# Attention with a routed feed-forward on one core: a value bank for each half of the queries

## The chip, the core and the metric

The kernel runs on one core of a Trainium2 chip. The time is the device time of one execution in microseconds; the figure for a kernel is the median of its runs. TensorE (PE in the profile) does matmuls and transposes, VectorE (DVE) and ScalarE (ACT) work on the results, GpSimd (POOL) does small work and indirect transfers, and SyncE (SP) issues most of the transfers. Matmul results land in PSUM, which is divided into banks of 512 fp32 values per partition.

## What is computed

Attention over 8 batches of 8 heads, 576 rows and 64 columns, in which each row keeps only the scores within `tau` of its maximum; then a mixture of 8 experts, in which every expert takes up to 576 rows by a greedy choice over all gate logits:

```python
def _attn_ref(q, k, v, tau):
    scale = 1.0 / np.sqrt(q.shape[-1])
    scores = scale * np.matmul(q, k.transpose(0, 1, 3, 2))
    thresh = np.max(scores, axis=-1, keepdims=True) - tau
    scores = np.where(scores >= thresh, scores, -1000000000.0)
    scores = scores - np.max(scores, axis=-1, keepdims=True)
    attn = np.exp(scores)
    attn = attn / (np.sum(attn, axis=-1, keepdims=True) + 1e-09)
    return np.matmul(attn, v).astype(np.float32)
...
def _moe_ref(x, w_gate, w1, w2):
...
    for e in range(E):
        mask = assigned == e
        h = np.maximum(x[mask] @ w1[e], 0.0)
        out[mask] = h @ w2[e]
```

## The kernel before, in words

The program has an attention stage, a short passage in which the router's first search runs beside the last gathered rows, and eight rounds of the expert feed-forward. The change lies in the attention stage and in the order of work right behind it.

**Pairs, tiles, slots.** Two heads of a batch make a pair: 32 pairs, four to a batch. A pair has nine tiles: eight of 128 query rows of one head, and a ninth that holds the last 64 rows of both heads. The 288 tiles go through a pipeline written out by hand in the loop over slots (lines 287 to 315); a slot starts two tiles, so nine slots handle two pairs and 18 slots a batch. In one slot the following are issued, each for the two tiles that have come that far:

- TensorE: scores (`score`, line 69) into a tile `sc` of two banks, one per tile; there are two such tiles, so the scores of a slot need the readers of the slot before to be done. At the slot's end the transposes of the weighted rows (`tr` and `turn`, line 98) into `tb`, of which there is one.
- VectorE: `mx` (line 74) reads the scores, writes `z` and the row's extreme; then `stt` (line 90) masks and sums the rows of the two tiles from a slot earlier.
- ScalarE: `trev` (lines 113 and 115) copies the transposed rows of the slot before to `pt`, then `ex` (line 86) takes the exponentials of this slot's `z`.

**Value units.** The output of a pair is formed in two halves of the query columns, 256 and 320 wide (`FQ`). A half takes four value units (`pv_unit`, line 144, two matmuls each) that accumulate into a bank `xo`, and the leftover matmuls (`pl_unit`, line 152) that finish both halves; ScalarE copies both banks to `xt` (line 153) in the next slot. The leftover matmuls need the leftover keys in `pl`: ten small transposes per pair (`left`, line 117, by `turn`) into unused columns of the score tiles, and four copies by ScalarE (`leftev`, lines 123 to 127).

**Whole units.** When the four pairs of a batch are done, `finish` puts four gate units (`lg_unit` twice, lines 171 and 173; `lgt_unit`, 183; `lgm_unit`, 193) into the list `aux`, and for the first two batches five row units as well (`xt_unit`, line 205: four transposes of `xt`, a copy and a store). The rows of the other batches wait until after the stage, in `late`. Each takes a bank `xo`, and its results are read by ScalarE or VectorE in the next slot.

**What sets the order.** Both kinds share a pool of two banks (`ps_v`, line 32). `columns` (line 257) takes value units from the queue, evenly over the slots that are left to a pair (`last_slot`); it doesn't open a pair's first half while whole units are waiting and no half is open, with exceptions. `whole` (line 271) issues up to two whole units in a slot, but only while no half is open:

```python
    def free_v(): return len(banks)<2 or banks[-2][0]
...
                if first and (not free_v() or (not all and not XO and len(aux)>(3 if p%2 else 0) and st["held"]!=p)): return
...
        while n<2 and aux and not XO and free_v() and st["slot"]>=st["last"]+aux[0][0]:
```

In the slot after a pair's ninth tile was transposed, all ten leftover transposes are issued: six behind the first tile's scores, four behind the second's, and ScalarE's four copies of them stand ahead of both exponentials.

Of the kernel before, what the change touches and what calls it, by code (L numbers as in the profile page):

```python
# [22 lines left out]
def attention(ctx, tc, qk, vl, tau, wgd, xrows, xts, Lg, nb_batches, ident, swap, R, after_first):  # L23
# [8 lines left out]
    ps_v=ctx.enter_context(tc.tile_pool(name="ps_v",bufs=2,space=PSUM))  # L32
# [89 lines left out]
    def leftev(p,n):  # L122
        if n==0: a=LB.pop((p,0)); A.activation(PL[p][:,0:384].rearrange("p (g r q) -> p r g q",g=3,r=2),a[:,:,HS:HS+192].rearrange("p r (g q) -> p r g q",g=3),AF.Copy)  # L123
        if n==0: return
        b=LB.pop((p,1))
        A.activation(PL[p][:,384:512].rearrange("p (r q) -> p r q",r=2),b[:,:,HS:HS+64],AF.Copy)
        for r in range(2): A.activation(PL[p][64-64*r:128-64*r,512:576],b[64-64*r:128-64*r,r,HS+64:HS+128],AF.Copy)  # L127
# [5 lines left out]
    banks=[]; VB={}  # L133
    def bank_v(sh):
        t=ps_v.tile(sh,F32,name="xo"); banks.append([False]); VB[id(t)]=banks[-1]
        return t
    def free_v(): return len(banks)<2 or banks[-2][0]
    def pv_unit(p,f,u):
        b,j=divmod(p,4)
        if b not in XT: XT[b]=wk.tile([128,4,S],F32,name="xt",bufs=XTB)  # L140
        if u==0: XO[p,f]=bank_v([128,512])
# [3 lines left out]
    def pl_unit(p,fs=(0,1)):  # L145

        b,j=divmod(p,4); r=[]
        for f in fs:
            xo=XO.pop((p,f)); q=FQ[f]; n=q.stop-q.start
            for a in range(2):  # L150
                g=slice(64*a,64*a+64); h=a^f
                T.matmul(xo[64*h:64*h+64,:n],LD[p]["v"][g,f,512:576],PL[p][g,q],start=False,stop=True,skip_group_check=True)  # L152
            r.append((VB[id(xo)],lambda xo=xo,q=q,n=n: A.activation(XT[b][:,j,q],xo[:,:n],AF.Copy)))
        have[p,"pv"]=1
        return r
    def bank_g(b,sh):
        if b<nb_batches-1: return bank_v(sh)
# [43 lines left out]
    def xt_unit(b,c):  # L201
        ps=bank_v([128,4,128])
# [20 lines left out]
    queue=[]; aux=[]; later=[]; late=[]; late2=[]; st={"last":-9,"slot":0,"held":-1}  # L223
    def push_pair(p):
        b,j=divmod(p,4)
        def when(n): return lambda: have.get((p,n),1<<30)+HOLD<=st["slot"]
        if p==NP-1:
# [4 lines left out]
            for f in range(2):  # L232
                for u in range(4): queue.append(("c",when("t3" if f==0 else "t8"),u==0,lambda f=f,u=u: pv_unit(p,f,u),p))
# [3 lines left out]
            queue.append(("n",lambda: not later,False,lambda: late.extend([lambda c=c: xt_unit(b,c) for c in range(5)]),p))  # L237
            return
        for f in range(2):
            for u in range(4): queue.append(("c",when("t3" if f==0 else "t8"),u==0,lambda f=f,u=u: pv_unit(p,f,u),p))  # L240
# [5 lines left out]
    def finish(b):  # L246
        aux.extend([(0,lambda: lg_unit(b,0)),(0,lambda: lg_unit(b,1)),(1,lambda: lgt_unit(b)),(0,lambda: lgm_unit(b))])
        rows=[lambda c=c: xt_unit(b,c) for c in range(5)]
# [7 lines left out]
    def last_slot(p): return 9*(p//2)+(12 if p%2 else 8)  # L256
# [700 lines left out]
```

## Time and profile before

| | us |
|---|---|
| median of three runs (1012.51 to 1014.81) | 1012.78 |
| the profiled execution | 1014.5 |
| its span, from the first to the last instruction | 1012.7 |
| busy in the span: PE, DVE, ACT, POOL | 960.3, 784.7, 639.1, 258.7 |
| first and last row-maximum instruction of attention start | 5.4, 468.9 |

The page gives busy times of each engine; groups of instructions by source line with their count, busy time, mean length and the idle time of their engine just before them; and who waited for whom. In the timeline the first column is the start and the second the length, both in us from the span's start, then the engine, the line, the operation, what is written and read, and how many were merged. A bracket gives the idle time before and what ended it. PEld is TensorE's weight load, which runs beside its matmuls.

### The profile page before, as it was taken

What the parts mean: (1) busy time and instruction counts of PE and PEld (TensorE: products, weight loads), DVE (VectorE), ACT (ScalarE), POOL (GpSimd) and SP (SyncE); (2) the same over time, 40 slices, a digit from 0 to 9 for tenths busy, and PEclk for the clock granted to TensorE, in tenths of its full rate; (3) what the DMA queues carried; (4) which work ended last, traced back from release to release, by engine and by line L of the source; (5) the groups of instructions that cost most, each with busy time, mean ns of one, the idle gap of its engine ahead of it and who ended that gap; (6) DMA issues with size and microseconds to landing.
All of it is one profiled execution on the core that took longest, in us unless ns stands there. A gap on an engine that the chain in (4) does not pass through costs nothing.

```text
span 1012.7 us, 24106 instructions
## 1 busy us (share of the span) xinstructions
PE 960.3 (95%) x9141; PEld 704.5 (70%) x9141; DVE 784.7 (77%) x2158; ACT 639.1 (63%) x1257; POOL 258.7 (26%) x411
## 2 busy tenths in 40 slices
PE   7999999999999999999879999999999899999996
PEld 4555555555555555555669789797887879899895
DVE  7999999999999899997578788788687687525220
ACT  6898889788988889897745344254352444535340
POOL 2333433333333333232020222221221203220202
PEclk9999999999999999999979999999999999999999
DMA  6332424233432323202770523434343415351101
GB/s 247 98 116 83 140 81 157 99 135 124 169 115 95 102 101 118 95 26 88 245 250 13 170 97 121 136 114 128 124 138 115 143 50 177 93 174 53 42 11 41
DMA packets 35859, 116.99 MB, mean 116 GB/s; under 512 B 4384, under 2 KB 5024, under 8 KB 35232
## 3 DMA queue, kind: packets, MB, share of 16 engines
q1 hardware_dynamic: 28352, 92.85, 26.8%
q0 software_dynamic: 5888, 19.03, 6.0%
q10 hardware_dynamic: 1504, 3.59, 1.2%
q8 instruction: 72, 1.18, 0.5%
q14 instruction: 43, 0.35, 0.1%
HBM read 93.01 MB, written 21.38 MB: 113 GB/s over the span
## 4 chain that ended last, share of the span: by engine, by line
PE 69%; DVE 12%; ACT 10%; issue 6%; DMA 2%; another core or an unknown queue 0%; DVEq 0%; POOLq 0%; SPq 0%; ACTq 0%
PE pf L787 21%; PE pf L819 19%; PE xo L144 8%; PE sc L69 8%; PE tb L98 6%; DVE z L74 4%; ACT pp L86 4%; DVE pp L90 3%; ACT pt L113 3%; PE xo L152 2%; PE pt L732 2%; ACT pl L127 1%; PE rps L440 1%; PE xo L205 1%; DMA out_dram<-y,idx 1%
## 5 line engine op out<-in xcount | busy, mean ns | idle before, releaser
L75 POOL TENSOR_SCALAR nb<-nb,taub 128x1 f32<-128x1 f32 x288 | 149.4, 519 | 308.3 <-DVE z L74 257.6
L74 DVE TENSOR_SCALAR_CACHE_REDUCE z<-sc 128x576 f32<-128x576 f32 x288 | 205.9, 752 | 26.8 <-PE sc L69 14.1
L86 ACT ACTIVATE pp<-z,nb 128x576 f32<-128x576 f32 x256 | 186.4, 771 | 23.6 <-DVE z L74 23.6
L90 DVE SCALAR_TENSOR_TENSOR pp<-z,nb,pp 128x576 f32<-128x576 f32 x256 | 199.9, 813 | 0.3
L819 PE MATMUL pf<-w2h,H 128*128 128x512 f32 x576 | 195.3, 402 | 0.7 <-DVE H L372 0.7
L69 PE MATMUL sc<-qk 64*128 64x288 f32 (+1 forms) x1280 | 186.4, 427 | 7.2 <-ACT pl L123 2.7
L144 PE MATMUL xo<-pt,vt 128*64 128x320 f32 (+1 forms) x1024 | 151.1, 418 | 3.4 <-PE sc L69 1.2
L113 ACT ACTIVATE pt<-tb 128x512 f32<-128x512 f32 x256 | 139.0, 588 | 5.2 <-PE tb L98 2.2
L819 PE MATMUL pf<-w2l,H 128*128 128x512 f32 x320 | 128.3, 401 | 0.0
L826 POOL DMA_INDIRECT out_dram<-y,idx x40 | 44.6, 1115 | 314.6 <-ACT y L822 238.6
L98 PEld LDWEIGHTS tb<-ident,pp 64*128 64x128 f32 x2048 | 75.0, 139 | 69.6 <-ACT pt L113 28.0
L819 PEld LDWEIGHTS pf<-w2h,H 128*128 128x128 f32 x576 | 106.5, 189 | 20.2 <-DVE H L372 1.6
L69 PEld LDWEIGHTS sc<-qk 64*128 64x128 f32 (+1 forms) x1280 | 91.1, 178 | 34.3 <-ACT pl L127 9.0
L787 PE MATMUL pf<-xh,w1h 128*128 128x288 f32 (+2 forms) x512 | 110.7, 303 | 0.7 <-ACT xh L733 0.7
L144 PEld LDWEIGHTS xo<-pt,vt 128*64 128x64 f32 x1024 | 63.4, 136 | 68.4 <-issue 34.7
L787 PE MATMUL pf<-xh,w1l 128*128 128x288 f32 (+2 forms) x512 | 110.7, 302 | 0.0
L787 PE MATMUL pf<-xl,w1h 128*128 128x288 f32 (+2 forms) x512 | 110.6, 302 | 0.0
L98 PE MATMUL tb<-ident,pp 64*128 64x64 f32 x2048 | 93.9, 229 | 12.3 <-ACT pt L113 12.0
L822 ACT ACTIVATE y<-pf 128x512 f32<-128x512 f32 x40 | 23.9, 598 | 129.3 <-PE pf L819 121.1
L799 ACT ACTIVATE hf<-pf 128x576 f32<-128x576 f32 x56 | 36.5, 652 | 93.2 <-PE pf L787 80.3
L787 PEld LDWEIGHTS pf<-xh,w1h 128*128 128x128 f32 x512 | 82.6, 191 | 1.5 <-ACT xh L733 1.1
L787 PEld LDWEIGHTS pf<-xh,w1l 128*128 128x128 f32 x512 | 82.6, 191 | 0.2
(199 smaller groups left out, 1311.4 us busy)
## 6 DMA issues: line engine op xcount, KB each, us to landing
qk<-qk_dram SPq DMA_DIRECT2D x31, 864.0 KB, 4.9
vt<-vl_dram SPq DMA_DIRECT2D x32, 576.0 KB, 3.8
w2s<-w_dram SPq DMA_DIRECT2D x32, 512.0 KB, 5.3
w1s<-w_dram SPq DMA_DIRECT2D x28, 512.0 KB, 4.3
xrows<-pp SPq DMA_DIRECT2D x24, 260.0 KB, 2.3
xts<-xt SPq DMA_DIRECT2D x2, 1152.0 KB
pt<-xts SPq DMA_DIRECT2D x2, 1152.0 KB, 7.9
xrows<-xr SPq DMA_DIRECT2D x8, 260.0 KB, 2.4
```

What stands on the lines that cost most here:

```text
L69: T.matmul(sc[o,f,:HS], kd["q",h][r,c], kd["k",h][r,:],start=True,stop=True)
L74: V.tensor_scalar(z,SC.pop(t)[:,:,:HS],-0.125,None,op0=ALU.mult,op1=ALU.min,accum_out=nb[:,0:1])
L75: G.tensor_scalar(nb[:,1:2],nb[:,0:1],taub[:,0:1],None,op0=ALU.add)
L86: A.activation(pview(t),ZB[t].rearrange("p a b -> p (a b)"),AF.Exp,bias=NBI[t][:,0:1],scale=-1.0)
L90: V.scalar_tensor_tensor(pv,ZB.pop(t).rearrange("p a b -> p (a b)"),NBI[t][:,1:2],pv,op0=ALU.is_le,op1=ALU.mult,accum_out=den_of(p)[:,p%4, ...
L98: g=slice(64*r,64*r+64); T.transpose(o[:,r],x[r%len(x)][g],ident[g,g])
L113: A.activation(PT[p][:,i%2,:,(i//2)*128:(i//2+1)*128].rearrange("p k (r q) -> p r k q",r=2),tb,AF.Copy)
L144: T.matmul(xo[64*h:64*h+64,:q.stop-q.start],v[:,f,128*u+64*h:128*u+64*h+64],PT[p][:,h,u,q],start=(u==0),stop=False,skip_group_check=True)
L787: T.matmul(ps[:,h,:n],s[w][:,k,f*128:(f+1)*128],s[x][:,k,cols[h]],start=(i==0),stop=(i==11))
L799: A.activation(hf,ps[:,:,:HS],AF.Relu)
L819: T.matmul(ps[:,0,:],H[:,f,c:c+128],s[w][:,f],start=(f==0 and j==0),stop=e)
L826: G.indirect_dma_start(out=out,out_offset=IOA(ap=s["idx"][:n,t:t+1],axis=0),in_=y[:n],in_offset=None)
```

## The change

- Each half has its own bank: `xo0` for the first, `xo1` for the second, one buffer each, with a list of flags for each. A first unit waits only for its own bank to be copied out; the hold-back for waiting whole units is gone.
- Whole units take the second half's bank, at most one in a slot, whenever it is free: beside value units of the first half.
- The leftover transposes go in two parts: six in the slot in which the ninth tile is transposed, four a slot later, both behind the scores of both tiles, in the second score tile. ScalarE's copies stand between the two exponentials.
- At the end, the last two pairs are spread over one slot less; in the slots without scores, the transposes go ahead of the value units. The late rows take the two banks in turn.

The names a to i stand for the nine slots of two pairs, counted from the slot in which the leftover keys of the first pair's ninth tile are at the stage of transposition: a and b hold the first pair's leftover transposes after the change (b all ten before), e and f the second pair's (f all ten before), and e and i the leftover matmuls.

```diff
-    ps_v=ctx.enter_context(tc.tile_pool(name="ps_v",bufs=2,space=PSUM))
+    ps_v=ctx.enter_context(tc.tile_pool(name="ps_v",bufs=1,space=PSUM))
...
     def leftev(p,n):
-        if n==0: a=LB.pop((p,0)); A.activation(PL[p][:,0:384]...
-        if n==0: return
-        b=LB.pop((p,1))
+        sc=LB.pop((p,n))
+        if n==0:
+            A.activation(PL[p][:,0:384]...
+            return
...
-    def free_v(): return len(banks)<2 or banks[-2][0]
+    banks=([[True]],[[True]])
+    def bank_v(sh,n):
+        banks[n].append([False])
+        return ps_v.tile(sh,F32,name="xo%d"%n)
+    def free_v(n): return banks[n][-1][0]
...
-        if u==0: XO[p,f]=bank_v([128,512])
+        if u==0: XO[p,f]=bank_v([128,512],f)
...
-        if b<nb_batches-1: return bank_v(sh)
+        if b<nb_batches-1: return bank_v(sh,1)
...
-    def xt_unit(b,c):
-        ps=bank_v([128,4,128])
+    def xt_unit(b,c,k=1):
+        ps=bank_v([128,4,128],k)
...
-    def last_slot(p): return 9*(p//2)+(12 if p%2 else 8)
+    def last_slot(p): return 9*(p//2)+(12 if p%2 else 8 if p<NP-2 else 7)
...
-                if first and (not free_v() or (not all and not XO and len(aux)>(3 if p%2 else 0) and st["held"]!=p)): return
+                if first and not free_v(first-1): return
...
     def whole():
-        n=0
-        while n<2 and aux and not XO and free_v() and st["slot"]>=st["last"]+aux[0][0]:
-            r=aux.pop(0)[1](); n+=1; st["last"]=st["slot"]
-            if queue: st["held"]=queue[0][4]
-            later.append((banks[-1],r))
+        if aux and free_v(1) and st["slot"]>=st["last"]+aux[0][0]:
+            r=aux.pop(0)[1](); st["last"]=st["slot"]
+            later.append((banks[1][-1],r))
...
-        p8=[t//9 for t in ev_ if t%9==8]
-        for n in range(2):
-            if n<len(sc_): score(sc_[n])
-            for p in p8: left(p,n,sc_[n] if n<len(sc_) else None)
+        p8=[(t//9,n) for n,x in enumerate((tr_,ev_)) for t in x if t%9==8]
+        for t in sc_: score(t)
+        for p,n in p8: left(p,n,sc_[-1] if sc_ else None)
...
-        for n in range(2):
-            for p in p8: leftev(p,n)
-        for t in sc_: ex(t)
+        for t in sc_[:1]: ex(t)
+        for p,n in p8: leftev(p,n)
+        for t in sc_[1:]: ex(t)
...
-        columns(); whole()
+        if sc_: columns(); whole()
         for t in tr_: tr(t,t==tr_[0])
+        if not sc_: columns(True); whole()
...
-            now=at; late.pop(0)()(); at=now+XTY
+            now=at; late.pop(0)(len(late)%2)(); at=now+XTY
```

TensorE's instructions in slots a and b of the sixth batch's gate units, before (`sc` scores and, written by `ident`, leftover transposes; `xo` with `wg` and `swap` gate units, with `vt` value units; `tb` transposes of the weighted rows):

```order
L69 MATMUL sc<-qk 128x288 x4
L171 MATMUL xo<-xt,wg 32x256 x4
L173 MATMUL xo<-rd,swap 128x4
L171 MATMUL xo<-xt,wg 32x320 x4
L98 MATMUL tb<-ident,pm_100 128x64 x8
L98 MATMUL tb<-ident,pp 128x64 x8
L69 MATMUL sc<-qk 128x288 x2
L98 MATMUL sc<-ident,pp 128x64 x6
L69 MATMUL sc<-qk 128x288 x2
L98 MATMUL sc<-ident,pp 128x64 x2
L98 MATMUL sc<-ident,pm_100 128x64 x2
L144 MATMUL xo<-pt,vt 64x256 x4
```

The same two slots after the change (lines are shifted by two behind the new code; the numbers tell the two banks' tiles apart):

```order
L69 MATMUL sc<-qk 128x288 x4
L98 MATMUL sc<-ident,pp 128x64 x6
L146 MATMUL xo_5886<-pt,vt 64x256 x2
L173 MATMUL xo_5890<-xt,wg 32x256 x4
L175 MATMUL xo_5890<-rd,swap 128x4
L98 MATMUL tb<-ident,pm_100 128x64 x8
L98 MATMUL tb<-ident,pp 128x64 x8
L69 MATMUL sc<-qk 128x288 x4
L98 MATMUL sc<-ident,pp 128x64 x2
L98 MATMUL sc<-ident,pm_100 128x64 x2
L146 MATMUL xo_5886<-pt,vt 64x256 x4
L173 MATMUL xo_5953<-xt,wg 32x320 x4
```

Slot a now has the first value unit and six leftover transposes, and one gate unit instead of two; slot b has four leftover transposes instead of ten, and the second gate unit.

ScalarE's instructions around the leftover copies of an odd pair (slot f), before (`xt` value copies, `pt` transposed rows, `pl` leftover copies, `pp` exponentials):

```order
L153 ACTIVATE xt<-xo 128x256
L153 ACTIVATE xt<-xo 128x320
L113 ACTIVATE pt<-tb 128x2x4x64
L115 ACTIVATE pt<-tb 128x8x64
L123 ACTIVATE pl<-sc 128x2x3x64
L126 ACTIVATE pl<-sc 128x128
L127 ACTIVATE pl<-sc 64x64 x2
L86 ACTIVATE pp<-z,nb 128x576 x2
```

And after, from the exponentials of slot e to those of slot f:

```order
L86 ACTIVATE pp<-z,nb 128x576
L125 ACTIVATE pl<-sc 128x2x3x64
L86 ACTIVATE pp<-z,nb 128x576
L155 ACTIVATE xt<-xo_831 128x256
L155 ACTIVATE xt<-xo_930 128x320
L113 ACTIVATE pt<-tb 128x2x4x64
L115 ACTIVATE pt<-tb 128x8x64
L86 ACTIVATE pp<-z,nb 128x576
L127 ACTIVATE pl<-sc 128x128
L128 ACTIVATE pl<-sc 64x64 x2
L86 ACTIVATE pp<-z,nb 128x576
```

The large copy moved a slot ahead, and both parts stand behind the first exponential.

TensorE's instructions at the end of the stage, from the last scores on, before:

```order
L69 MATMUL sc<-qk 64x288 x4
L144 MATMUL xo<-pt,vt 64x256 x4
L98 MATMUL tb<-ident,pp 128x64 x16
L144 MATMUL xo<-pt,vt 64x320 x4
L98 MATMUL tb<-ident,pp 128x64 x16
L144 MATMUL xo<-pt,vt 64x320 x4
```

And after:

```order
L69 MATMUL sc<-qk 64x288 x4
L146 MATMUL xo_7349<-pt,vt 64x320 x4
L98 MATMUL tb<-ident,pp 128x64 x32
L146 MATMUL xo_7349<-pt,vt 64x320 x4
```

Four value matmuls of the first half went ahead of the last scores, and two slots' transposes now follow each other.

More of the change, by code (lines that the diff above doesn't have):

```diff
@@ L217, in xt_unit @@
         return ev
-    queue=[]; aux=[]; later=[]; late=[]; late2=[]; st={"last":-9,"slot":0,"held":-1}
+    queue=[]; aux=[]; later=[]; late=[]; late2=[]; st={"last":-9,"slot":0}
     def push_pair(p):
@@ L232, in push_pair @@
             for f in range(2):
-                for u in range(4): queue.append(("c",when("t3" if f==0 else "t8"),u==0,lambda f=f,u=u: pv_unit(p,f,u),p))
+                for u in range(4): queue.append(("c",when("t3" if f==0 else "t8"),0 if u else f+1,lambda f=f,u=u: pv_unit(p,f,u),p))
                 if f==0: queue.append(("n",when("t8"),False,lambda: rd_calc(b),p))
@@ L282, in attention @@
     after_first()
-    ps=ps_v.tile([128,512],F32,name="xo")
+    ps=bank_v([128,512],0); banks[0][-1][0]=True
     def idles(n):
```

18 lines of the change are left out of this document (7 added, 11 removed).

## The prediction

> **What bounds the kernel now.** I read the groups of instructions first, then the waits, then the stretches, then the timeline of the attention stage, where all of the change lies. VectorE's group for the row maxima (`z`, line 74), from the page:
>
> ```profile
> L74 DVE TENSOR_SCALAR_CACHE_REDUCE z<-sc 128x576 f32<-128x576 f32 x288 | 205.9, 752 | 26.8 <-PE sc L69 14.1
> ```
>
> Behind the bar stands 26.8 us of idle time ahead of these 288 instructions. The waits (engine, line, awaited: us in total, times, longest) name its causes and two more that matter below:
>
> ```profile
> DVE z L74 <- PE sc L69: 14.1, 21, 3.4
> DVE z L74 <- PE sc L98: 11.6, 15, 0.8
> ACT pl L123 <- DVE z L74: 24.0, 29, 2.1
> PE tb L98 <- ACT pt L113: 12.7, 32, 1.0
> ```
>
> `z` waits for scores (L69), or for the leftover transposes (L98 into `sc`); TensorE's own transposes wait 32 times, 0.4 us on average, for ScalarE. One stretch of 40 us in the stage (busy us of each engine, granted clock, DMA):
>
> ```profile
> 380.00:420.00 40.00, 37.74 (x449) 21.98 (x449) 37.14 (x104) 35.29 (x66) 11.81 (x24) 1.00 0.32 101
> ```
>
> TensorE 37.74, VectorE 37.14 and ScalarE 35.29 of 40 us, at full clock: three engines nearly full, with two or three microseconds lost in each 40. None is the bound all the time; TensorE and VectorE alternate. The timeline of two slots (start, us, engine) shows how:
>
> ```profile
> 356.12 0.71 PE L98 MATMUL tb<-ident,pp 64*128 64x64 f32 x16
> 356.66 1.19 PE L69 MATMUL sc<-qk 64*128 64x288 f32 x8
> 357.42 0.76 DVE L74 TENSOR_SCALAR_CACHE_REDUCE z<-sc 128x576 f32<-128x576 f32 x1
> 357.78 1.30 PE L144 MATMUL xo<-pt,vt 128*64 128x320 f32 x8
> 359.01 0.77 PE L152 MATMUL xo<-pl,vt 64*64 64x256 f32 x8
> 359.71 0.71 ACT L153 ACTIVATE xt<-xo 128x256 f32<-128x256 f32 x2
> 359.71 0.46 PE L98 MATMUL tb<-ident,pp 64*128 64x64 f32 x8
> 360.26 0.70 PE L69 MATMUL sc<-qk 64*128 64x288 f32 x4
> 360.80 0.34 PE L98 MATMUL sc<-ident,pp 64*128 64x64 f32 x6
> 360.98 0.70 PE L69 MATMUL sc<-qk 64*128 64x288 f32 x4
> 361.18 0.76 DVE L74 TENSOR_SCALAR_CACHE_REDUCE z<-sc 128x576 f32<-128x576 f32 x1 [0.84 <-PE sc L98]
> 361.52 0.22 PE L98 MATMUL sc<-ident,pp 64*128 64x64 f32 x2
> 361.73 1.08 PE L144 MATMUL xo<-pt,vt 128*64 128x256 f32 x8
> 362.04 0.49 ACT L123 ACTIVATE pl<-sc 128x384 f32<-128x384 f32 x1 [0.49 <-DVE z L74]
> 362.75 0.71 PE L98 MATMUL tb<-ident,pp 64*128 64x64 f32 x16
> 363.29 1.19 PE L69 MATMUL sc<-qk 64*128 64x288 f32 x8
> ```
>
> TensorE is packed, so costs are start to start (the trace counts each fp32 matmul that is no transpose twice: x8 is four). Scores of two tiles: 357.78-356.66 = 1.12. Transposes of two tiles: 356.66-356.12 = 0.54 (0.55 below). Four value matmuls of the second half 359.01-357.78 = 1.23, of the first half 362.75-361.73 = 1.02. Leftover value matmuls (L152) 359.71-359.01 = 0.70. Leftover transposes: six 0.18 (360.80 to 360.98), four 0.21 (361.52 to 361.73). `z` starts 357.42-356.66 = 0.76 after the scores when it waits for them. At 361.18 it has waited 0.84 us: the slot before was 3.6 us of TensorE work, and the six transposes ran between its own scores and it. ScalarE's `pl` copy at 362.04 comes before the exponentials, and holds the score tile it reads.
>
> Gate units on TensorE (L171 and L173; then L183 and L193):
>
> ```profile
> 374.20 0.64 PE L171 MATMUL xo<-xt,wg 128*32 128x256 f32 x8
> 374.77 0.39 PE L173 MATMUL xo<-rd,swap 128*128 128x4 f32 x2
> 375.08 0.74 PE L171 MATMUL xo<-xt,wg 128*32 128x320 f32 x8
> 375.76 0.46 PE L98 MATMUL tb<-ident,pm 64*128 64x64 f32 x8
> 344.73 0.66 PE L183 MATMUL xo<-ident,lt 128*128 128x128 f32 x4
> 345.42 0.46 PE L98 MATMUL tb<-ident,pm 64*128 64x64 f32 x8
> ```
>
> The first gate unit costs 0.57+0.31 = 0.88, the second 0.68, the two transposed ones 0.69 (about 0.49 and 0.20). On VectorE:
>
> ```profile
> 366.89 0.17 DVE L164 TENSOR_SCALAR rd<-den 128x36 f32<-128x36 f32 x1
> 367.40 0.70 DVE L74 TENSOR_SCALAR_CACHE_REDUCE z<-sc 128x576 f32<-128x576 f32 x1
> 370.24 0.76 DVE L74 TENSOR_SCALAR_CACHE_REDUCE z<-sc 128x576 f32<-128x576 f32 x1
> 376.68 0.36 DVE L178 COPY rm<-rd 64x4 f32<-64x4 f32 x2
> 377.42 0.76 DVE L74 TENSOR_SCALAR_CACHE_REDUCE z<-sc 128x576 f32<-128x576 f32 x1
> 347.21 0.48 DVE L188 TENSOR_TENSOR lw<-xo,rd 128x128 f32<-128x128 f32 x2
> 348.69 0.74 DVE L74 TENSOR_SCALAR_CACHE_REDUCE z<-sc 128x576 f32<-128x576 f32 x1
> 137.28 1.09 PE L205 MATMUL xo<-ident,xt 128*128 128x128 f32 x8
> 139.75 1.28 DVE L213 COPY xr<-xo 128x512 f32<-128x512 f32 x2
> ```
>
> A slot without extras takes VectorE 370.24-367.40 = 2.84. Each batch adds the reciprocal 0.51 (366.89 to 367.40), the `rm` copies 0.74 (376.68 to 377.42) and the logits 1.48 (347.21 to 348.69): 2.73. A row unit takes TensorE 1.09/2 = 0.55 and VectorE 1.28/2 = 0.64; ten of them run inside the stage. The ends of the stretch that I sum, slots 16 and 142 of the 144:
>
> ```profile
> 50.74 0.75 DVE L74 TENSOR_SCALAR_CACHE_REDUCE z<-sc 128x576 f32<-128x576 f32 x1
> 461.09 0.76 DVE L74 TENSOR_SCALAR_CACHE_REDUCE z<-sc 128x576 f32<-128x576 f32 x1 [0.67 <-PE sc L69]
> ```
>
> 126 slots, seven batches of 18, in 410.35 us, or 58.6 a batch. VectorE's work in it is 126x2.84 + 7x2.73 + 10x0.64 = 383.4 us; the other 27.0 are waits.
>
> **The change part by part.** No matmul, copy or exponential is added or dropped in these slots; what changes is which slot holds them. I name the nine slots of two pairs a to i, as in the section on the change. TensorE's work, with 1.67 for scores and transposes in each:
>
> Before, without gates: a 1.67, b 3.08 (ten leftover transposes, 1.02), c 2.69, d 2.90, e 1.67+1.23+0.70 = 3.60, f 3.08, g 2.69, h 2.90, i 3.60. All gate units lie in a (1.56 or 0.69) or, where the hold-back misses, in f together with those transposes.
>
> After: a 1.67+0.18+0.51 = 2.36, b 1.67+0.21+1.02 = 2.90, c 1.67+0.51+0.62 = 2.80, d 2.90, e 1.67+0.18+0.62+0.70 = 3.17, f 2.90, g 2.69, h 2.90, i 3.60. Gate units go to a (0.88), b (0.68), f (0.49), g (0.20), one in each.
>
> The sums are equal; the spread is not. TensorE can run ahead of VectorE by only 2.84-0.76-0.76 = 1.3 us, since the two score tiles must be read before they are refilled, and lead beyond that is lost. Tally of the lead through a changed batch, starting at none; each slot adds VectorE's time less TensorE's, and what would go under zero is a wait. Gate half: a 2.84-3.24 = -0.40, wait 0.40; b 2.84+0.74-3.58 = 0; c +0.04; d -0.06, wait 0.02; e -0.33, wait 0.33; f 2.84-3.39 = -0.55, wait 0.55; g 2.84+1.0-2.89 = +0.95; h +0.42, to the cap 1.3; i -0.76, to 0.54. Other half: a +0.48, b -0.06, c +0.04, d -0.06, e -0.33, f -0.06, g +0.15+0.51 and h -0.06 leave 1.15, i 0.39. That lead then covers the next batch's a, all but 0.01, so a settled batch waits 0.01+0.02+0.33+0.55 = 0.91 us and takes 18x2.84 + 2.73 + 0.91 = 54.8. TensorE's own sum is 28.5+26.2 = 54.7: it would be dense. The two batches with row units add 5x0.55 to TensorE: 57.4, and VectorE has 57.1; I take 57.6. Seven batches: 5x54.8 + 2x57.6 = 389.2, against 410.35: **21.2 us less**.
>
> The leftover copies. Their transposes now stand behind both score tiles, in the second. So the first `z` of a slot no longer waits for them, and of the two score tiles only the second waits for ScalarE. The second `z` starts at the earliest 0.76+0.76 = 1.52 after the scores began, the six transposes end at 1.12+0.34 = 1.46: no wait. The page of the Trainium skill "PSUM — Partial Sum Buffer", section "PSUM bank collisions raise a hardware error", asks for accesses of two engines to be kept apart by bank, not by address. By it the transposes still share a bank with what `z` reads, and only the 0.06 us above keeps the saving whole; the trace agrees that they are kept apart, with `z` at 361.18 behind transposes that end at 360.80+0.34 = 361.14.
>
> What I keep back. ScalarE is busy 35.29 of 40 us, some 2.5 of a slot of 2.9, and slot f has the two `xt` copies (0.71) and the rest of `pl` on top, so the transposes of slot g may still wait for it as they do now (0.4 us, once a pair). The waits for `pl` ahead of the scores go, so I leave half of that 0.4, 0.2 us, in 16 slots: 3.2 us. From nothing (21.2 stays) to all 12.7 us as now (8.5 stays). **I take 18.0 us.**
>
> Row units. Each leaves with its own VectorE copy in the next slot, 0.64, where two came together; POOL's part and the store go along. On SP's queue the stores now stand between other loads, but those loads are issued a pair or more ahead. Nothing, at most 10x0.64 within what the tally holds.
>
> The end. The value matmuls of one group (1.02) move ahead of the last scores, and one set of transposes ahead of the value matmuls. The row there:
>
> ```profile
> 472.25 0.71 PE L98 MATMUL tb<-ident,pp 64*128 64x64 f32 x16 [0.35 <-ACT pt L113]
> ```
>
> TensorE waits 0.35 for ScalarE even with those matmuls ahead of it, so without them it waits longer: from nothing to 1.02, I take **0.3**. Late rows alternate between two banks as they did, and the router's search behind them is the same chain; it starts earlier by what the stage saves.
>
> The sum: the profiled execution took 1014.5 us (span 1012.7) and stands 1.7 over the median of 1012.78. 1014.5-18.3 = 996.2 for it; **994.5 us** for the median.
>
> **The rivals.** A measurement of this kernel can tell about 0.3% (3 us) from no change.
>
> *ScalarE becomes the bound.* Its 12.7 us of holding TensorE's transposes stay in full, since `pl` copies now sit between two exponentials. For it: 35.29 of 40 busy. Against: the queue gets shorter where it was longest. 21.2-12.7 = 8.5 gained: 1004.3 us.
>
> *Slower: one bank for each half.* Before, groups rotated over two banks; now the next group of a half must wait for its own bank's copy, and all transposes and scores queue behind it on TensorE. A bank's two `xt` copies take 0.71, at most 0.36 on average for one. If all 64 group starts, 28 gate units and 10 row units waited as long as a copy, 102x0.36 = 37 us are lost: 994.5+37 = 1031 us, and it turns the balance at 18.3/102 = 0.2 us each. Against: in the rows above the copies end at 359.71+0.71 = 360.42, and the next group starts at 361.73, 1.3 us later. It decides only if ScalarE falls 1.3 us further behind. The Trainium skill's "Perfetto Trace Analysis", section "Matmuls", says that independent groups should rotate through banks so that the copy-out overlaps the next group: by that rule the change goes the wrong way within a half. The trace bears it out only as far as groups of one half followed each other directly, which they don't.
>
> *Nothing gained.* VectorE is full, and the lead that TensorE gains is spent in slots where VectorE has its extras. Its 27.0 us of waits speak against; for it, the lead is capped at 1.3 us. Within 3 us: 1012 us.
>
> *All of it and more.* No wait for ScalarE is left, and the start and the end give 1 to 3 us besides: 989 us.
>
> **How the numbers follow.** Forecast (990 to 999 us) 0.70; ScalarE as the bound (999 to 1009.7) 0.15; more (under 990) 0.07; nothing 0.04; slower 0.04. Faster: 0.70+0.15+0.07 = 0.92, same 0.04, slower 0.04. The range reaches from 988.5, where nearly all of the fourth case is in, to 1005, just past the ScalarE case.
>
> **What would show it.** Right: the 126 slots take about 392 us; idle time ahead of `z` falls from 26.8 to 10 us or less, with L98 gone from its causes; slot f no longer opens with a wait of 0.8; slot i (3.6 us of TensorE work) is the longest left; everything behind the stage keeps its length. Wrong: `xo` matmuls waiting for `xt` or `lt` copies (the bank rival); transposes still waiting 12 us for `pt` (ScalarE); or a stage that is shorter while the search behind it is longer.

## The result, and the profile after

The changed kernel takes **999.6 us** in the median of four runs (998.47 to 1003.83), beside 1013.79 for the kernel before on the same chip: a ratio of 0.9867, 95% interval 0.9833 to 0.9901, so 14.2 us less. Four more runs beside the last experiments gave 0.9868 (0.9831 to 0.9905). The forecast was 18.3 us less, 994.5 us; 999.6 lies inside the stated range (988.5 to 1005) and just above the band of 990 to 999 us that had the chance of 0.70. The profiled execution took 1003.83 us (span 1001.9) and is the slowest of its four. In the experiments below, one execution of the leftovers alone took 3088 us, the others 1001 to 1005; its ratio leaves that one out.

From the page, the groups of `z` and of the value matmuls after the change:

```profile
L74 DVE TENSOR_SCALAR_CACHE_REDUCE z<-sc 128x576 f32<-128x576 f32 x288 | 205.7, 750 | 14.6 <-PE sc L69 13.8
L146 PE MATMUL xo<-pt,vt 128*64 128x320 f32 (+1 forms) x1024 | 155.7, 420 | 0.4 <-DVE xr L215 0.3
```

The idle time ahead of `z` fell from 26.8 to 14.6 us, and the leftover transposes (L98) are no longer among its causes. TensorE sat idle ahead of value matmuls for 0.4 us in all, so a bank for each half costs next to nothing. The waits after (engine, line, awaited: us in total, times, longest):

```profile
ACT pp L86 <- DVE z L74: 39.1, 82, 3.4
DVE z L74 <- PE sc L69: 13.8, 27, 3.5
PEld sc L69 <- ACT pl L128: 5.3, 13, 0.6
PE tb L98 <- ACT pt L113: 5.1, 7, 1.3
```

TensorE's transposes wait 7 times for ScalarE where they waited 32 times, 5.1 us instead of 12.7. `pl` waiting for `z` (24.0 us) is gone from the top; ScalarE's exponentials now wait for `z` instead, 39.1 us where it was 23.6. The weight loads of the scores still wait for the second leftover copy (`pl`, L128), which holds the second score tile, but less than in the kernel before, where its line was L127:

```profile
PEld sc L69 <- ACT pl L127: 9.0, 19, 0.6
```

A stretch of 40 us in a batch without row units (busy us of PE, PEld, DVE, ACT, POOL; granted clock; DMA):

```profile
370.00:410.00 40.00, 39.95 (x483) 23.73 (x477) 39.44 (x112) 36.09 (x72) 12.80 (x26) 1.00 0.35 113
```

TensorE is busy 39.95 of 40 where it was 37.74, and VectorE 39.44 where it was 37.14. The stretch that the prediction summed, and the end of the stage, by starts of `z` in slots 16, 142 and 143:

```profile
50.47 0.75 DVE L74 TENSOR_SCALAR_CACHE_REDUCE z<-sc 128x576 f32<-128x576 f32 x1
447.76 0.76 DVE L74 TENSOR_SCALAR_CACHE_REDUCE z<-sc 128x576 f32<-128x576 f32 x1 [0.23 <-PE sc L69]
450.63 0.76 DVE L74 TENSOR_SCALAR_CACHE_REDUCE z<-sc 128x576 f32<-128x576 f32 x1
```

The 126 slots take 397.29 us instead of 410.35: 13.06 less, where 18.0 were forecast. The same 126 slots before and after, with the columns of the 40 us above:

```profile
50.74:461.09 410.35, 395.56 (x4732) 231.10 (x4732) 386.30 (x1092) 360.64 (x689) 136.30 (x269) 1.00 0.32 108
50.47:447.76 397.29, 396.44 (x4737) 232.66 (x4735) 385.62 (x1097) 354.66 (x687) 143.67 (x269) 1.00 0.33 112
```

TensorE's idle time there fell from 14.8 us to 0.85. Batch by batch (18 slots, from slot 25 on) 58.09, 58.48, 57.50, 55.87, 55.75, 55.86: the first three hold the ten row units, the others none. The forecast was 57.6 for a batch with row units, 54.8 without.

The first and the last of the leftover rows at the end, TensorE after the change, and the two rows of before that they compare with:

```profile
455.19 0.71 PE L98 MATMUL tb<-ident,pp 64*128 64x64 f32 x16
457.08 0.71 PE L98 MATMUL tb<-ident,pp 64*128 64x64 f32 x16 [1.18 <-ACT pt L113]
...
461.39 0.46 PE L98 MATMUL tb<-ident,pp 64*128 64x64 f32 x8 [1.34 <-ACT pt L113]
...
466.48 0.77 PE L154 MATMUL xo<-pl,vt 64*64 64x256 f32 x8
```

```profile
465.41 0.74 DVE L74 TENSOR_SCALAR_CACHE_REDUCE z<-sc 128x576 f32<-128x576 f32 x1
479.80 0.77 PE L152 MATMUL xo<-pl,vt 64*64 64x256 f32 x8
```

From `z` of slot 143 to the last leftover value matmuls it is 466.48-450.63 = 15.85 us, before 479.80-465.41 = 14.39: 1.46 us more. In sum the last leftover value matmul comes 13.32 us sooner: 0.27 before slot 16, 13.06 in the stretch, 1.45 in slot 142 (4.32 before, 2.87 now), less 1.46.

Behind it the same instructions follow in both kernels, 532.90 us before and 535.42 after in the profiled executions. In the experiments that leave that part alone it is 528.4 to 536.7 us, so a single execution can be 8 us off there, and I compare kernels by the stretch and the end. In the two profiled executions of the changed kernel these agree to 0.1 us.

### The profile page after: what moved, and what is told of

Read it like the earlier page. It is cut to its first block, busy times and chain, and to the rows that moved or that the text cites. A ratio compares the mean times of both kernels' runs of the same rounds, so it can differ in the third digit from the quotient of the medians.

```text
span 1001.9 us, 24115 instructions
## 1 busy us (share of the span) xinstructions
PE 964.3 (96%) x9141; PEld 710.4 (71%) x9141; DVE 781.2 (78%) x2158; ACT 633.0 (63%) x1257; POOL 261.9 (26%) x411
## 3 DMA queue, kind: packets, MB, share of 16 engines
q8 instruction: 72, 1.18, 0.5%
## 4 chain that ended last, share of the span: by engine, by line
PE 84%; DVE 8%; issue 3%; DMA 2%; ACT 1%; another core or an unknown queue 0%; POOLq 0%; SPq 0%; DVEq 0%; ACTq 0%
PE pf L787 21%; PE pf L819 19%; PE sc L69 13%; PE xo L146 13%; PE tb L98 8%; DVE pp L90 2%; PE xo L154 2%; PE pt L732 2%; DVE z L74 2%; PE xo L207 1%; PE rps L440 1%; PE xo L173 1%; DMA out_dram<-y,idx 1%; PE sc L98 1%; DVE cmp L372 1%
## 5 line engine op out<-in xcount | busy, mean ns | idle before, releaser
L75 POOL TENSOR_SCALAR nb<-nb,taub 128x1 f32<-128x1 f32 x288 | 152.6, 530 | 286.2 <-DVE z L74 235.5
L86 ACT ACTIVATE pp<-z,nb 128x576 f32<-128x576 f32 x256 | 193.3, 774 | 39.6 <-DVE z L74 39.1
L74 DVE TENSOR_SCALAR_CACHE_REDUCE z<-sc 128x576 f32<-128x576 f32 x288 | 205.7, 750 | 14.6 <-PE sc L69 13.8
L69 PE MATMUL sc<-qk 64*128 64x288 f32 (+1 forms) x1280 | 181.2, 427 | 3.4 <-DVE z L74 1.5
L146 PE MATMUL xo<-pt,vt 128*64 128x320 f32 (+1 forms) x1024 | 155.7, 420 | 0.4 <-DVE xr L215 0.3
L69 PEld LDWEIGHTS sc<-qk 64*128 64x128 f32 (+1 forms) x1280 | 93.8, 179 | 33.7 <-DVE z L74 5.7
L98 PEld LDWEIGHTS tb<-ident,pp 64*128 64x128 f32 x2048 | 75.4, 139 | 58.0 <-ACT pp L86 20.1
L146 PEld LDWEIGHTS xo<-pt,vt 128*64 128x64 f32 x1024 | 60.7, 136 | 57.7 <-issue 27.4
L98 PE MATMUL tb<-ident,pp 64*128 64x64 f32 x2048 | 94.1, 229 | 5.0 <-ACT pt L113 4.8
```

The costliest lines, as they stand in the source:

```text
L69: T.matmul(sc[o,f,:HS], kd["q",h][r,c], kd["k",h][r,:],start=True,stop=True)
L74: V.tensor_scalar(z,SC.pop(t)[:,:,:HS],-0.125,None,op0=ALU.mult,op1=ALU.min,accum_out=nb[:,0:1])
L75: G.tensor_scalar(nb[:,1:2],nb[:,0:1],taub[:,0:1],None,op0=ALU.add)
L86: A.activation(pview(t),ZB[t].rearrange("p a b -> p (a b)"),AF.Exp,bias=NBI[t][:,0:1],scale=-1.0)
L98: g=slice(64*r,64*r+64); T.transpose(o[:,r],x[r%len(x)][g],ident[g,g])
L146: T.matmul(xo[64*h:64*h+64,:q.stop-q.start],v[:,f,128*u+64*h:128*u+64*h+64],PT[p][:,h,u,q],start=(u==0),stop=False,skip_group_check=True)
```

## The experiments

Each table entry is a difference of two starts in the trace of one profiled execution: the stretch from `z` of slot 16 to `z` of slot 142, a batch without row units (slots 115 to 133), and the end (`z` of slot 143 to the last leftover value matmul). Ratios are to the kernel before, run on the same chip. The batch is a fair sample after the change (55.75 to 55.87 us for three of them); before, the batches without row units range from 57.5 to 60.7, and with the leftovers alone from 56.4 to 58.7.

| kernel | stretch | batch | end | ratio, 95% interval |
|---|---|---|---|---|
| before | 410.35 | 58.50 | 14.39 | 1 |
| changed kernel | 397.29 | 55.86 | 15.85 | 0.9867 (0.9833 to 0.9901) |
| changed kernel again | 397.35 | 55.88 | 15.85 | 0.9868 (0.9831 to 0.9905) |
| old end | 397.36 | 55.88 | 13.20 | 0.9833 (0.9809 to 0.9858) |
| banks alone | 401.38 | 56.66 | 13.86 | 0.9894 (0.9866 to 0.9922) |
| leftovers alone | 399.89 | 56.77 | 13.73 | 0.9878 (0.9851 to 0.9905) |
| short tile as a full one | 393.90 | 55.41 | 15.68 | 0.9828 (0.9799 to 0.9857) |
| other order in the short tile | 397.34 | 55.88 | 13.20 | 0.9818 (0.9795 to 0.9840) |
| all rows late | 390.59 | 55.88 | 13.19 | 0.9896 (0.9874 to 0.9919) |
| leftover transposes twice | 404.16 | 56.89 | 13.19 | 0.9900 (0.9879 to 0.9922) |
| copies first | 405.37 | 57.20 | 13.86 | 0.9933 (0.9910 to 0.9955) |
| ten in one slot | 405.11 | 57.38 | 13.58 | 0.9925 (0.9899 to 0.9951) |
| copies last | 402.81 | 56.98 | 13.68 | 0.9906 (0.9871 to 0.9942) |
| more on VectorE | 399.16 | 56.17 | 13.22 | 0.9836 (0.9802 to 0.9871) |

**The end undone.** The order at the end as it was:

```diff
-    def last_slot(p): return 9*(p//2)+(12 if p%2 else 8 if p<NP-2 else 7)
+    def last_slot(p): return 9*(p//2)+(12 if p%2 else 8)
...
-        if sc_: columns(); whole()
+        columns(); whole()
         for t in tr_: tr(t,t==tr_[0])
-        if not sc_: columns(True); whole()
```

> The changed kernel, with the order at the end of the attention stage as it was before (value matmuls ahead of each set of transposes while no scores are left). Theory: in the changed kernel TensorE's transposes at the end wait 1.18 and 1.34 us for ScalarE, because no value matmuls stand ahead of them; with the old order about 1.0 to 1.5 us of that goes. From the first z of slot 143 to the last leftover value matmul: 14.4 to 14.9 us instead of 15.85; the total about 1.2 us under the changed kernel (0.12%). Rival (the prediction's step): the new order costs only 0.3 us, or nothing, and the longer end has another cause: 15.5 us or more.

The stretch is the same to 0.1 us, and the end is 13.20 us, 2.65 less than with the new order and 1.2 less than in the kernel before. The theory holds, and its size was too small. One wait is left (TensorE, with the old order):

```profile
454.51 0.71 PE L98 MATMUL tb<-ident,pp 64*128 64x64 f32 x16
455.15 1.30 PE L146 MATMUL xo<-pt,vt 128*64 128x320 f32 x8
456.65 0.71 PE L98 MATMUL tb<-ident,pp 64*128 64x64 f32 x16 [0.21 <-ACT pt L113]
```

Four value matmuls stand between the two sets of transposes, and cover the copy of the first set. Two waits of 1.18 and 1.34 became one of 0.21.

**Each part alone.** First the banks: `left` and `leftev` are called as in the kernel before, the end too. Then the leftovers: in the kernel before, these lines of the change and no other:

```diff
-        p8=[t//9 for t in ev_ if t%9==8]
-        for n in range(2):
-            if n<len(sc_): score(sc_[n])
-            for p in p8: left(p,n,sc_[n] if n<len(sc_) else None)
+        p8=[(t//9,n) for n,x in enumerate((tr_,ev_)) for t in x if t%9==8]
+        for t in sc_: score(t)
+        for p,n in p8: left(p,n,sc_[-1] if sc_ else None)
...
-        for n in range(2):
-            for p in p8: leftev(p,n)
-        for t in sc_: ex(t)
+        for t in sc_[:1]: ex(t)
+        for p,n in p8: leftev(p,n)
+        for t in sc_[1:]: ex(t)
```

> A bank for each half, with gates and rows in the second one beside value units; leftover transposes in one slot behind each score tile, their copies ahead of both exponentials, and the end as before. Theory (the spread of TensorE's work over the slots sets the waits, and both parts level it): about two thirds of the 14.2 us, 1003 to 1006 us; z waits again for the leftover transposes (some 10 us in the stage), and slots with a gate unit and ten transposes (3.76 of TensorE work) are the longest. Rival 1: the banks give everything, about 999 us. Rival 2: the banks give little, 1010 us or more, and the gain comes from the leftovers.

> The kernel before, with only the leftover transposes in two parts, both behind the second score tile, and their copies between the exponentials. Theory: some 5 to 8 us less than before, 1005 to 1009 us; L98 is gone from the causes of z's waits, but the slots with two gate units stay. Rival 1: everything comes from this part, about 999 us. Rival 2: nothing, 1012 us or more, since the gate units still pile up on the same slots.

The banks alone shorten the stretch by 8.97 us, the leftovers alone by 10.46, both by 13.0. So neither gives all, and 6.4 us are in both. That would fit slots that had gate units, ten transposes and ScalarE's copies together, which either part breaks up; no run shows it slot by slot. The banks alone took 1004.4 us, as the theory had it. The leftovers alone gave 12 us by the ratio, more than the 5 to 8 expected; L98 is gone from the causes of `z`'s waits, and its waits behind scores grew from 14.1 to 19.7 us. Some 10 us of `z` waiting for the leftover transposes were expected with the banks alone; this is what its waits show instead:

```profile
DVE z L74 <- PE sc L69: 13.6, 23, 3.5
ACT pl L125 <- DVE z L74: 13.4, 26, 1.3
...
DVE z L74 <- PE sc L98: 3.1, 10, 0.3
```

Only 3.1 us of it is left; what is worse than in the changed kernel is the copies' wait for `z`.

**What TensorE's sum lacked.** The ninth tile's scores as two full matmuls (its output leaves these rows out):

```diff
-        else: todo=((0,slice(0,64),slice(512,576)),(1,slice(64,128),slice(512,576)))
+        else: todo=((0,slice(0,128),slice(448,576)),)
```

> The changed kernel; the scores of each pair's ninth tile (the last 64 queries of both heads, four matmuls of 64x64x288) are left out, and two full matmuls of 64x128x288 (head 0, queries 448 to 575) stand there instead, so its output is not the reference's. Theory: TensorE is dense in the changed kernel's batches without row units (55.8 us), and what my tally missed there is the short tiles, whose score matmuls take 0.16 to 0.21 us more than a full tile's and the transposes ahead of them 0.09 more, 0.92 us a batch. Without them a batch without row units takes 54.9 to 55.1 us, the stretch from slot 16 to slot 142 about 391 us instead of 397.3, and the total falls by 6 to 7.5 us. Rival: the missing 1.0 us a batch is lead lost by ScalarE's copies or by the two score tiles; then it falls by less than 2 us.

What this rests on, three rows of TensorE around an ordinary slot and a slot with a ninth tile in the changed kernel:

```profile
387.12 0.71 PE L98 MATMUL tb<-ident,pp 64*128 64x64 f32 x16
387.66 1.19 PE L69 MATMUL sc<-qk 64*128 64x288 f32 x8
388.79 1.30 PE L146 MATMUL xo<-pt,vt 128*64 128x320 f32 x8
...
410.66 0.71 PE L98 MATMUL tb<-ident,pp 64*128 64x64 f32 x16
411.30 1.40 PE L69 MATMUL sc<-qk 64*64 64x288 f32 x12
412.63 1.30 PE L146 MATMUL xo<-pt,vt 128*64 128x320 f32 x8
```

Start to start, transposes and scores take 0.54+1.13 in the first, 0.64+1.33 in the second. In the experiment a batch takes 55.41 us and the stretch 393.90: 3.4 us less, between the theory's 6.3 and the rival's 2. In the trace of this run the price is gone from the rows: in the batch from slot 115 the transposes take 0.55 us in every slot, and the scores 1.12 in two of the four slots that had the short tile (in the other two they hold waits). But only half of the 0.92 us a batch is given back, because with less work TensorE waits more: idle for 0.36 of the 55.41 us, where it was 0.05 of 55.86. The waits:

```profile
DVE z L74 <- PE sc L69: 11.5, 24, 3.5
PEld sc L69 <- ACT pl L128: 4.9, 13, 0.6
PE xo L146 <- DVE lwm L200: 1.4, 5, 0.4
PE xo L146 <- DVE xr L215: 1.0, 2, 0.6
```

What grew is the wait of value matmuls for VectorE to read a gate or row unit out of the shared bank, 7 times, 2.4 us instead of 0.3. The loads for the scores wait 13 times for the copy that holds the second tile, about as before.

**Another order in the short tile**, from here on always with the old end:

```diff
-        for h,o,c in todo:
-            for f in range(2):
-                r=slice(64*f,64*f+64)
-                T.matmul(sc[o,f,:HS], kd["q",h][r,c], kd["k",h][r,:],start=True,stop=True)
+        for f in range(2):
+            for n,(h,o,c) in enumerate(todo):
+                f_=f^n; r=slice(64*f_,64*f_+64)
+                T.matmul(sc[o,f_,:HS], kd["q",h][r,c], kd["k",h][r,:],start=True,stop=True)
```

> The changed kernel with the old end; the four score matmuls of each pair's ninth tile in another order, the same results: each next one goes to other rows and, in the second step, to other columns of the array (head 0 first half, head 1 second half, head 0 second half, head 1 first half). Theory: their extra time over a full tile (0.16 to 0.21 us) comes from neighbours on the same columns, so it falls by up to 0.2 us a pair; as with full matmuls in their place, the stretch from slot 16 to 142 falls by up to 3.4 us, to 394, and the total from 998.3 to about 995. Rival: the extra time belongs to the form (four weight loads instead of two), and the order changes nothing: stretch 397 to 397.7.

Nothing: 397.34. The rival holds; as far as this one other order shows, the price belongs to the form of the matmuls, not to who stands next to whom.

**The row units.** `NBO=2` becomes `NBO=4`.

> The changed kernel with the old end; the row units of the first two batches too go through DRAM and run behind the attention stage, so that no row unit runs inside it. Theory: each of the ten row units costs about 0.66 us in the stage (the three batches in which they lie are 6.6 us longer in sum than three others), so the stretch from slot 16 to 142 falls by 6 to 6.6 us, to about 391; behind the stage the late rows, 1.05 us each, reach some 10 us further, to about 505 us from the start, past the first gather of rows at 503 us, so up to 4 us are given back: 992 to 996 us. Rival: the search behind the stage, in which TensorE is 73 to 85% busy, takes the full price of them, 8 us or more: 998 us or slower.

The stretch falls by 6.77 us, 0.68 for each row unit, and every batch now takes 55.7 to 55.9. But the part behind the stage takes 546.51 us instead of 529.53 in the profiled executions: 17 us are lost there, for 6.8 gained. By the medians it is some 14.6: 1003.62 us, beside 995.74 for the run with the other order in the short tile, on the same chip. The rival holds. The first gather of rows is issued at 500.59 us instead of 500.32, so the search with ten more row units beside it ate all of the lead; and the first expert's matmuls begin at 513.73 instead of 508.56, after a wait of 2.23 us for `xh`. Why that grew was not followed.

**Which engine is the bound now.** Leftover transposes done twice, and, by itself, a small VectorE operation in every second slot:

```diff
         for p,n in p8: left(p,n,sc_[-1] if sc_ else None)
+        for p,n in p8*(len(sc_)//2): left(p,n,sc_[-1])
```

```diff
         for t in tt_: stt(t)
+        if s_%2==0 and sc_: V.tensor_scalar(more,more,1.0,None,op0=ALU.mult)
```

> The changed kernel with the old end; all leftover transposes inside the stage are done twice, with the same results: 0.18 and 0.21 us more of TensorE's work for each pair, 1.56 us a batch, 10.9 us in the seven batches from slot 16 to 142. Theory: TensorE is dense in the changed kernel's attention stage, with about 0.5 us a batch to spare, so the stretch grows by 7.5 to 11 us, to 405 to 408, and the total by 9 to 12 us. Rival: VectorE or ScalarE is the bound now and TensorE has room: the stretch grows by less than 4 us.

> The changed kernel with the old end, and one more VectorE operation of 128x36 (as the first of the reciprocal's two, 0.17 to 0.21 us) in every second slot of the attention stage: 1.9 us a batch, 13 us in the stretch from slot 16 to 142. Theory: VectorE has 2.0 us a batch to spare by its sum (53.85 of 55.87), but the two engines take turns: doubled transposes took 6.8 of 10.9 us, so here a part shows too, 2 to 7 us. Rival 1: TensorE alone is the bound: under 1 us. Rival 2: VectorE is the bound: 11 us or more.

More on TensorE, 10.9 us, takes 6.80 us more (62%); more on VectorE, 13 us, takes 1.80 (14%). Both came out a little under the theories' ranges. But these shares rest on prices that were too high, as the rows show. Six transposes and what follows them, with the old end and then done twice; and VectorE's added operation where nothing waits:

```profile
392.14 0.34 PE L98 MATMUL sc<-ident,pp 64*128 64x64 f32 x6
392.42 0.65 PE L146 MATMUL xo<-pt,vt 128*64 128x256 f32 x4
...
397.79 0.53 PE L98 MATMUL sc<-ident,pp 64*128 64x64 f32 x12
398.25 0.65 PE L146 MATMUL xo<-pt,vt 128*64 128x256 f32 x4
```

```profile
394.76 0.17 DVE L311 TENSOR_SCALAR more<-more 128x36 f32<-128x36 f32 x1
394.85 0.74 DVE L74 TENSOR_SCALAR_CACHE_REDUCE z<-sc 128x576 f32<-128x576 f32 x1
```

Start to start, the six cost 0.46 instead of 0.28 when done twice, and the four 0.34 instead of 0.21: 0.31 a pair and 8.7 us in the stretch, not 10.9, so 78% of it shows. VectorE's operation costs 0.09 us, not 0.2: 5.7 us in the stretch, not 13, so 32% shows. TensorE is the bound with next to nothing to spare (idle 0.05 us a batch, none with the transposes doubled); what doesn't show took the place of waits within its rows. VectorE's work counts for about a third.

**Where ScalarE's copies stand.** Ahead of both exponentials, or behind both:

```diff
-        for t in sc_[:1]: ex(t)
         for p,n in p8: leftev(p,n)
-        for t in sc_[1:]: ex(t)
+        for t in sc_: ex(t)
```

> The changed kernel with the old end; ScalarE's copies of the leftover transposes ahead of both exponentials instead of between them. Theory: these copies hold the second score tile (TensorE's weight loads for the scores wait 13 times, 5.3 us in all, for them); ahead of the exponentials they come up to 0.77 us sooner, so those waits go and the stretch falls by 1 to 3 us, to 394 to 396. Rival: then the copies hold up the first exponential instead, as in the kernel before, and the transposes and VectorE's next step behind it: the stretch grows by 1 to 5 us.

> The changed kernel with the old end; ScalarE's copies of the leftover transposes behind both exponentials. Theory: the second exponential comes 0.5 to 0.7 us sooner, but the copies hold the second score tile 0.77 us longer, beyond the 0.2 to 0.6 us that the weight loads of the scores wait for them now; so TensorE loses about 0.5 us a pair and a part of it is made up: the stretch grows by 3 to 10 us. Rival: only the place ahead of the first exponential hurts, and the stretch stays within 1 us of 397.4.

Ahead, the stretch grows by 8.01 us: the rival holds, and its 1 to 5 us were too small. Behind, by 5.45: the theory holds. The waits with the copies ahead:

```profile
ACT pl L125 <- DVE z L74: 30.2, 31, 1.1
...
ACT pp L86 <- DVE z L74: 16.2, 29, 3.3
PE tb L98 <- ACT pt L113: 8.2, 23, 1.0
```

And one slot there, rows of ScalarE, VectorE and TensorE:

```profile
413.06 0.49 ACT L125 ACTIVATE pl<-sc 128x384 f32<-128x384 f32 x1 [1.00 <-DVE z L74]
413.45 1.43 ACT L86 ACTIVATE pp<-z,nb 128x576 f32<-128x576 f32 x2
```

```profile
411.53 0.76 DVE L74 TENSOR_SCALAR_CACHE_REDUCE z<-sc 128x576 f32<-128x576 f32 x1
412.21 0.75 DVE L74 TENSOR_SCALAR_CACHE_REDUCE z<-sc 128x576 f32<-128x576 f32 x1
```

```profile
411.80 0.34 PE L98 MATMUL sc<-ident,pp 64*128 64x64 f32 x6
```

The copy starts at 413.06, right after the second `z` ends (412.96), although its transposes were done at 412.14; the first exponential could have run from the end of the first `z` (412.29), and comes over 1 us late, at 413.45, with everything behind it. Between the exponentials that wait is filled with the first of them. The page of the Trainium skill "PSUM — Partial Sum Buffer", section "PSUM bank collisions raise a hardware error", asks for any two engines' accesses to one bank to be kept apart, reads against reads too; the trace agrees with such a wait, 31 times, 1.0 us each. With the copies behind both exponentials, the other side shows:

```profile
PEld sc L69 <- ACT pl L128: 13.4, 24, 1.2
PEld sc L69 <- ACT pl L125: 7.4, 15, 1.4
```

The score tile comes free later, 20.8 us of waiting instead of 6.8 in the changed kernel (5.3 for L128, 1.5 for L125).

**Ten transposes in one slot**, six into the first score tile, four into the second, copies between the exponentials:

```diff
-        p8=[(t//9,n) for n,x in enumerate((tr_,ev_)) for t in x if t%9==8]
+        p8=[(t//9,n) for t in ev_ if t%9==8 for n in range(2)]
...
-        for p,n in p8: left(p,n,sc_[-1] if sc_ else None)
+        for p,n in p8: left(p,n,sc_[n] if n<len(sc_) else None)
```

> The changed kernel with the old end, but all ten leftover transposes in one slot again, behind both scores, six into the first score tile and four into the second; their copies stay between the two exponentials. Theory: what the split into two slots is worth is small against the copies' place (with the copies ahead of both exponentials the stretch grew by 8.0 us): TensorE's work is the same in sum, and the two score tiles wait for three copies in a row; the stretch grows by 1 to 5 us, to 398.5 to 402.5. Rival (the prediction's reasoning by the spread of TensorE's work): the pile of 1.02 us in slot b, 3.76 with a gate unit, is what counts, and the stretch grows by 6 us or more.

The stretch grows by 7.75 us: the rival holds, and my theory falls.

```profile
DVE z L74 <- PE sc L98: 11.0, 20, 0.8
...
PEld sc L69 <- ACT pl L128: 9.3, 28, 0.4
PEld sc L69 <- ACT pl L125: 6.1, 14, 1.0
```

The first `z` waits for transposes again, and three copies in a row hold the score tiles. How much of the 7.75 is the pile of work and how much the first tile, this run doesn't separate.

**The changed kernel again**, unedited:

> The changed kernel once more, beside the others on one chip. Theory: the stretch from slot 16 to 142 is 397.3 us again, the end from the first z of slot 143 to the last leftover value matmul 15.85; what differs between runs of one kernel lies behind the stage, where the search and the expert layers run.

It holds: 397.35 and 15.85; behind the stage 530.19 us instead of 535.42.

The version to keep is the changed kernel with the old end. Its ratio and that of its twin with the other order in the short tile (0.9833 and 0.9818) lie below the changed kernel's 0.9867 and 0.9868. Their intervals overlap, so the times alone don't prove it; the 2.65 us at the end stand in the traces (15.85 in both of the changed kernel, 13.20 in both with the old end).

## Why the prediction was right, and where its sizes were off

- **Right: sign, mechanism and range.** The waits were where the prediction put them, and leveling TensorE's work over the slots took its idle time in the stretch from 14.8 to 0.85 us. Of `z`'s waits there, those behind leftover transposes (11.2 us) went; those behind scores stayed (9.0 before, 8.9 after).
- **Signs that failed.** Idle time ahead of `z` is 14.6 us, not 10 or less, and the 126 slots take 397.3, not 392. Slot f opens with a wait of 0.31 us, less than the 0.84 of before, but not none. The time itself fell in the band that the chances give to ScalarE as the bound (999 to 1009.7), and not for that reason.
- **A batch without row units: 54.8 forecast, 55.8 measured.** This is the term that failed: "TensorE's own sum is 28.5+26.2 = 54.7: it would be dense". It is dense (idle 0.05 us), but the sum was too small. Its largest error is 0.92 us: it took 1.12 us for the scores in each of 18 slots, where the four slots with a ninth tile take 1.28 or 1.33, and the transposes ahead of two of these 0.64. The other errors nearly cancel: value units and gate units cost about 0.4 us more than summed, waits within the rows are 0.27, and four leftover transposes behind both score tiles take 0.12 us, not 0.21, 0.36 less a batch. The row of a slot with a ninth tile stood in the trace of before as well; I took one slot's price for all. That trace also shows TensorE busy for 395.56 us in the 126 slots, more than the 392.4 forecast for all of their time. Seven batches at 1.03 are 7.2 us.
- **The lead.** "That lead then covers the next batch's a": it doesn't. Slot a opens with a wait of 0.55 us in each of the last batches, since the lead is spent on the ninth tiles, or never built while the second leftover copy holds a score tile; how much of each, the runs don't separate. The slot forecast as the longest, i (3.46), is passed by f (3.89, with VectorE's 1.0 of logits in it) and a (3.55).
- **Row units.** 5.6 us were forecast for the ten (two times 57.6-54.8), 6.8 measured by taking them out. They are spread over three batches, not two.
- **Kept back for ScalarE: 3.2 us, hardly needed.** The transposes wait 5.1 us for `pt`, 2.52 of that (1.18+1.34) at the end and 0.2 in the 126 slots. (The 12.7 of before, taken as the upper bound, is for the whole stage; 8.2 of it lies in these slots.) But the reason was luck in part: the prediction saw the copies between two exponentials as a danger, and did not price what their place is worth. Ahead of both they would have cost 8.0 us, and behind both 5.45. A gain of the size that the ScalarE rival had, 8.5 us, was one line of code away: with the copies ahead, the ratio is 0.9933, 6.8 us.
- **These terms close the stretch.** 7.2+0.9-3.2 = 4.9 us (0.9: 397.3 less seven batches of 55.83 leaves 6.5 us for the row units, less the 5.6), and 397.3 is 4.9 above the 392.4 that the prediction had.
- **The end: 0.3 us forecast, 1.46 measured, 2.65 against the old order.** The mechanism was right (the transposes wait longer for ScalarE). The bound of 1.02 was not: it counted one wait, and the new order makes two. The sign in the sum was wrong too: by the prediction's own words the 0.3 is a loss, but it is added to the gain; 18.0-0.3 = 17.7 would have given 995.1 us. That slot 142 became 1.45 us shorter, which makes up for the end, was in no term: luck.
- **One bank for each half.** The rival decides at 0.2 us a group; the value matmuls waited 0.4 us in all. "Perfetto Trace Analysis" of the Trainium skill, section "Matmuls", has independent groups rotate through banks. Here a fixed bank for each half serves as well: no value matmul waits for a copy. The margin is thinner than the 1.3 us of the prediction, though: the next group of a first half starts 0.07 to 2.0 us after the copy of the last ended, 0.76 in the middle of 31, and with the copies first value matmuls do wait for `xt`, 4 times, 1.4 us. With the leftovers in place, going from two shared banks to one for each half, and with it to whole units beside value units, shortens the stretch by 2.5 us (399.89 to 397.36); the runs don't separate the two.

## What to carry to other kernels

When the sum of one engine's work decides, price every form of its instructions that occurs in the period, each from its own row: one short form, four times in 18 slots, was the largest part of the miss here. Then hold the sum against that engine's busy time over the same slots in the trace. An experiment that adds work needs the same care: read from its own rows what the added instruction costs before taking a share. Small copies belong in the gap where their engine would wait anyway, and should be done before the next user needs the buffer they read; check both neighbours before moving them. Where no new work follows, keep independent work between two steps that hand a buffer back and forth.

## What the runs showed of the hardware

- Four score matmuls of 64x64x288 in place of two of 64x128x288 cost 0.16 to 0.21 us more in a pair of tiles, and another order changes nothing (397.34 against 397.36 us). "TensorEngine Tiling (Array Packing)" of the Trainium skill, section "Key Properties", says that a change of the array's tiling drains TensorE; the 0.64 instead of 0.54 us ahead of such a tile would fit, but no run here takes a change of tiling by itself.
- The stretch repeats to 0.1 us between executions (397.29 and 397.35), while the same instructions behind the stage took 528.4 to 536.7 us; the granted clock over the span was 0.991 in the profiled run of 529.5 and 0.983 in that of 536.7.
